# A seven-product second layer on all four experts of a fused attention and mixture-of-experts kernel on one Trainium2 core

## Chip, core and metric

The kernel runs on one core of one Trainium2 chip. The metric is the device time of one execution in microseconds (us), taken as the median of several executions. Executions of one kernel agree within about half a per cent. An experiment is always timed against the kernel before on the same chip in the same rounds. Its ratio is the mean time of its fast runs over the mean time of the fast runs of the kernel before of the same rounds, so it is not quite the ratio of the medians that I quote. A 95% interval stands beside it.

The *granted clock* is the share of PE's full clock that it was given.

The engines are called PE (TensorE: matmuls), DVE (VectorE), ACT (ScalarE), POOL (GpSimd) and SP (SyncE, which issues loads and stores). PE accumulates into PSUM banks, and DVE and ACT drain them.

## The reference

```python
def phi(x): return np.where(x > 0, x, np.exp(x) - 1.0) + 1.0     # elu + 1

q_p, k_p = phi(q), phi(k)                     # q, k, v: 8 batches x 8 heads x 576 tokens x 64
kv  = einsum('bhsd,bhse->bhde', k_p, v);  z = sum(k_p, axis=2)
x   = einsum('bhsd,bhde->bhse', q_p, kv) / (einsum('bhsd,bhd->bhs', q_p, z) + 1e-6)
x   = x.transpose(0, 2, 1, 3).reshape(4608, 512)
p   = domain_probs / domain_probs.sum(-1)
out = sum over 4 experts e of  p[:, e] * (relu(x @ w1[e]) @ w2[e])   # 512 -> 1024 -> 512
```

## The kernel before

Tokens are worked on in nine tiles of 512: each batch of 576 gives 512, and the eight left-over groups of 64 make up the last tile. A *unit* is one expert on one tile. Tile 0 and the first unit of tile 1 use plain matmuls. The other 31 units run in a software pipeline. Their first layer is cut into 2x2 sub-matrices and computed with **seven products instead of eight** (Strassen's scheme in Winograd's form). The price is sums of sub-matrices: of weights on DVE once, and of tokens on POOL for each tile. The second layer has the same scheme, but only on experts 0 and 2. I take the reason to be room: its three weight sums for each expert, 128x1024 fp16 each in the trace, take SBUF.

```python
SE = (0, 2)                                  # experts whose layer 2 is seven-product
...
def hidden_sums(h):                          # POOL: four sums for each half of the hidden units
    hs = pm.tile([P, 3, 2, NH], FP16, tag="hs", bufs=2, name="hs")
    nc.gpsimd.tensor_tensor(out=hs[:, 0], in0=a21, in1=a22, op=AO.add)
    ...
class Block:                                 # half a unit of layer 1: seven products in seven slots
    def p1(self):
        self.b = self.bank("b")
        self.products(self.b, ..., True)
        self.u1 = self.copy("u1", 1)         # ACT copies the bank to SBUF
    def p2(self):
        s2 = self.bank("s")                  # a bank of its own
        self.products(s2, ..., True)
        add_relu(self.h[:, :, 0, 0:NH], s2, self.u1)     # DVE: relu(bank + u1)
    ...
def phi_act(self, name, g, part=0, parts=1):
    ee = pa.tile([P, HG * CM * D], FP16, tag="phie", bufs=2, name="ee")  # exp goes to SBUF
    nc.scalar.activation(eeh, src, AF.Exp)
    if self.b > 2:
        nc.scalar.activation(dsth, src, AF.Identity, bias=1.0)           # x+1 on ACT
def phi_dve(self, name, g, part=0, parts=1):
    if self.b > 2:                           # one DVE instruction: min(max(x+1, 1), exp)
        nc.vector.scalar_tensor_tensor(out=dst, in0=dst, scalar=1.0, in1=ee, op0=AO.max, op1=AO.min)
    else:                                    # two: max(x+1, 1), then min with exp
        nc.vector.tensor_scalar(dst, src, 1.0, 1.0, AO.add, AO.max)
        nc.vector.tensor_tensor(out=dst, in0=ee, in1=dst, op=AO.min)
...
# in the pipeline, for each unit
if e in SE:
    l2 = [(layer2_product, j, e, hT, hss, p, i) for p in (2, 5, 1, 6, 7, 3, 4) for i in range(2)]
else:
    l2 = [... layer2_part ...]               # 32 plain matmuls of 512 columns, four DVE accumulations
```

Attention of the next batch (phi, kv, the division) is sprinkled between the products of a tile. So tile 1 carries the attention of the third batch (`b == 2`), and the last two tiles carry none.

## Time and profile before

| kernel before | |
|---|---|
| time before | 517.59 us median (515.88 to 517.7) |
| profiled execution, span | 514.0 us |
| PE busy | 96% |
| matmul work on PE, from start-to-start spacing | 487 us |
| PE stall between first and last matmul | 19 us |

From the page's first three parts: the header, busy time by engine, then PE's row and the granted clock in 40 slices of the span (9 means 90% or more). The fifth line is the chain that ended last.

```profile
span 514.0 us, 9987 instructions
PE 495.8 (96%) x3815; PEld 356.8 (69%) x3815; DVE 342.5 (67%) x676; ACT 289.0 (56%) x564; POOL 198.0 (39%) x207
PE   6899989999999999999999999999999999999996
PEclk9999999999999999999999999999999999999998
PE 85%; ACT 6%; DVE 3%; issue 2%; DMA 2%; POOL 0%; SPq 0%; DVEq 0%; ACTq 0%
```

PE is the bound: it is busy nearly everywhere. The two 6s at the ends are the start of the attention and the last stores.

Busy time includes the overlap of pipelined matmuls (the page gives a 512-column matmul a length of 379 ns), so I work with the spacing of starts. A long uninterrupted stretch of plain layer-2 matmuls is the cleanest ruler. This is the chain of waits in the last microseconds, with start, length and the number of instructions:

```profile
502.05 6.92 PE py L476 x32
```

This is 6.92 / 32 = 0.216 us for a matmul of 512 columns. The median spacing for 256 columns in this trace is 0.109 us. Everything above that spacing I call *stall*; where the records show the granted clock at half, I count the doubling apart as *clock* (eight matmuls of 256 columns took 1.71 us at half clock and 0.87 at full in the trace after).

In tile 1 PE waits for almost nothing; this is the whole answer of the wait view for PE in that stretch:

```profile
engine line waited for: us in total, times, longest us
PE psum_nl L380 <- DMA ql<-qlp: 0.5, 1, 0.5
```

Three groups of the page that the change touches: plain layer 2 (672 matmuls), the seven-product ones with a right-hand side from the weights (360), and the DVE add-ReLU after product 2 (`CUSTOM_DVE_ANT_0` is the page's name for the kernel's `add_relu`). Columns: line, engine, operation, out<-in, shape, count, busy us, mean ns, idle before.

```profile
L476 PE MATMUL py<-w,h 128*128 128x512 f16 x672 | 183.6, 379 | 0.3 <-DVE acc L467 0.3
L556 PE MATMUL py<-w,h 128*128 128x256 f16 x360 | 53.8, 272 | 2.8 <-ACT acc L465 2.7
L606 DVE CUSTOM_DVE_ANT_0 h<-ps,u 128x512 f16<-128x512 f32 x62 | 42.4, 684 | 6.5 <-PE ps L622 3.4
```

### The profile page before, as it was taken

The page shows a single profiled execution, that of the slowest core. Times are in us where ns is not written, and L with a number is a line of the kernel's source. Part 1 is how long each engine was busy: PE and PEld are TensorE (multiplying, and loading weights), DVE is VectorE, ACT ScalarE, POOL GpSimd, SP SyncE. Part 2 cuts the span into 40 slices and gives each one's busy share as a digit, 9 for nine tenths or more (in the row PEclk, how much of TensorE's full clock was granted, in tenths as well). Part 3 has the DMA queues.
Part 4 walks back from the last instruction along what each step waited for, and adds up shares of the span by engine and source line. Part 5 has one row for each costly group of instructions (what it writes and reads, how often), then busy time and mean ns, then how long its engine had stood idle before and what let it go on. Part 6 is the DMA issues. An engine that isn't in the chain of part 4 may idle for free.

```text
span 514.0 us, 9987 instructions
## 1 busy us (share of the span) xinstructions
PE 495.8 (96%) x3815; PEld 356.8 (69%) x3815; DVE 342.5 (67%) x676; ACT 289.0 (56%) x564; POOL 198.0 (39%) x207
## 2 busy tenths in 40 slices
PE   6899989999999999999999999999999999999996
PEld 2444445668787777778786868687778787878782
DVE  5614674689856885777677867687669555755573
ACT  5752465863876395737583668357843354335430
POOL 3522313016260736055423733372427251824240
PEclk9999999999999999999999999999999999999998
DMA  9999927573426334433435251523132110011003
GB/s 266 200 208 207 265 83 230 147 200 77 142 107 149 55 102 149 110 80 98 151 84 119 65 180 62 129 40 122 41 47 48 38 47 0 1 42 43 0 2 84
DMA packets 80193, 54.22 MB, mean 105 GB/s; under 512 B 45488, under 2 KB 73136, under 8 KB 80144
## 3 DMA queue, kind: packets, MB, share of 16 engines
q1 hardware_dynamic: 71104, 41.64, 30.5%
q0 software_dynamic: 9040, 11.93, 12.1%
q8 instruction: 30, 0.49, 0.4%
q14 instruction: 19, 0.16, 0.1%
HBM read 45.16 MB, written 9.44 MB: 106 GB/s over the span
## 4 chain that ended last, share of the span: by engine, by line
PE 85%; ACT 6%; DVE 3%; issue 2%; DMA 2%; POOL 0%; SPq 0%; DVEq 0%; ACTq 0%
PE py L476 27%; PE pb L622 19%; PE py L556 15%; PE pe L622 10%; PE ph L421 6%; PE ps L622 5%; ACT ee L226 2%; PE psum_kv L323 1%; ACT qp L228 1%; PE psum_nd L363 1%; DVE x_sb L346 1%; DMA rawb<-in_v_dram 1%; ACT acc L465 1%; DVE acc L467 1%; ACT u L633 1%
## 5 line engine op out<-in xcount | busy, mean ns | idle before, releaser
L476 PE MATMUL py<-w,h 128*128 128x512 f16 x672 | 183.6, 379 | 0.3 <-DVE acc L467 0.3
L467 DVE SCALAR_TENSOR_TENSOR acc<-py,p_sb,acc 128x256 f32<-128x256 f32 (+1 forms) x230 | 128.9, 567 | 41.3 <-PE py L556 24.4
L633 ACT COPY u<-pb 128x512 f32<-128x512 f32 x186 | 109.1, 588 | 79.6 <-PE pb L622 79.3
L606 DVE CUSTOM_DVE_ANT_0 h<-pe,u 128x512 f16<-128x512 f32 x124 | 85.3, 688 | 80.4 <-ACT u L633 47.4
L530 POOL TENSOR_TENSOR hs<-h 128x512 f16<-128x512 f16 x30 | 34.6, 1155 | 235.3 <-DVE h L606 235.3
L622 PEld LDWEIGHTS <-w 128*128 128x128 f16 x992 | 95.5, 98 | 33.4
L622 PEld LDWEIGHTS <-s 128*128 128x128 f16 x744 | 71.7, 98 | 24.8
L476 PEld LDWEIGHTS <-h 128*128 128x128 f16 x672 | 65.4, 98 | 30.1 <-issue 0.4
L666 ACT ACTIVATE h<-pb 128x512 f16<-128x512 f32 x62 | 37.1, 598 | 73.6 <-PE pb L622 73.4
L622 PE MATMUL pb<-tt,w 128*128 128x256 f16 x496 | 74.4, 273 | 0.0
L556 PE MATMUL py<-w,h 128*128 128x256 f16 x360 | 53.8, 272 | 2.8 <-ACT acc L465 2.7
L556 PEld LDWEIGHTS <-h 128*128 128x128 f16 x480 | 46.8, 98 | 10.3 <-issue 3.9
L606 DVE CUSTOM_DVE_ANT_0 h<-ps,u 128x512 f16<-128x512 f32 x62 | 42.4, 684 | 6.5 <-PE ps L622 3.4
L226 ACT ACTIVATE ee<-rawb 128x512 f16<-128x512 f32 (+1 forms) x54 | 37.1, 691 | 6.2 <-DMA rawb<-in_q_dram 6.0
L465 ACT ACTIVATE acc<-py,p_sb 128x256 f32<-128x256 f32 (+1 forms) x64 | 32.5, 507 | 12.2 <-PE py L556 6.7
L556 PEld LDWEIGHTS <-hs 128*128 128x128 f16 x360 | 35.2, 98 | 4.5 <-issue 0.3
L421 PE MATMUL ph<-xT,w 128*128 128x512 f16 x160 | 37.3, 379 | 0.8 <-ACT xT L400 0.7
L622 PE MATMUL pb<-tt,s 128*128 128x256 f16 x248 | 37.2, 273 | 0.0
L622 PE MATMUL pe<-tt,s 128*128 128x256 f16 x248 | 37.2, 273 | 0.0
L556 PE MATMUL py<-t,hs 128*128 128x256 f16 x240 | 35.9, 273 | 0.0
L531 POOL TENSOR_TENSOR hs<-hs,h 128x512 f16<-128x512 f16 x30 | 34.6, 1154 | 2.4
L532 POOL TENSOR_TENSOR h<-h 128x512 f16<-128x512 f16 x30 | 34.7, 1155 | 0.0
(97 smaller groups left out, 565.3 us busy)
## 6 DMA issues: line engine op xcount, KB each, us to landing
out_dram<-acc SPq DMA_DIRECT2D x32, 256.0 KB, 2.4
w<-in_moe_w_dram POOLq DMA_DIRECT2D x14, 512.0 KB, 19.8
rawb<-in_v_dram SPq DMA_DIRECT2D x13, 512.0 KB, 5.0
rawb<-in_q_dram SPq DMA_DIRECT2D x13, 512.0 KB, 3.9
rawb<-in_k_dram SPq DMA_DIRECT2D x13, 512.0 KB, 4.6
w<-in_moe_w_dram POOLq DMA_DIRECT2D x4, 256.0 KB, 6.8
rawb<-in_q_dram POOLq DMA_DIRECT2D x2, 512.0 KB, 6.1
rawb<-in_k_dram POOLq DMA_DIRECT2D x2, 512.0 KB, 4.7
```

The lines of the kernel that those rows point to most:

```text
L226: nc.scalar.activation(eeh, src, AF.Exp)
L421: nc.tensor.matmul(out=ph, lhsT=w1_sb[e][:, dc, fj * P : (fj + 1) * P], rhs=xT_of(j)[:, dc], start=(dc == 0), stop=(dc == DC - 1),)
L465: nc.scalar.activation(acc, ps, AF.Identity, scale=pscal)
L467: nc.vector.scalar_tensor_tensor(out=acc, in0=ps, scalar=pscal, in1=acc, op0=AO.mult, op1=AO.add)
L476: nc.tensor.matmul(out=py, lhsT=rows(hT, fj)[:, ns * P : (ns + 1) * P], rhs=w2_sb[e][:, fj, :], start=(fj == 0), stop=(fj == FC - 1),)
L530: nc.gpsimd.tensor_tensor(out=hs[:, 0], in0=a21, in1=a22, op=AO.add)
L532: nc.gpsimd.tensor_tensor(out=a21, in0=a11, in1=a21, op=AO.subtract)
L556: nc.tensor.matmul(out=ps, lhsT=lhsT(k), rhs=rhs[:, k], start=first and k == 0, stop=k == FH - 1, skip_group_check=True,)
L606: nc.vector._custom_dve(TENSOR_ADD_SAT, out=out, in0=ps, in1=u, s0=BIG, s1=0.0)
L622: nc.tensor.matmul(out=ps[:, kk], lhsT=lk(kc), rhs=rhs[:, kc], start=first and kk == 0 and kc == 0, stop=kc == 1, skip_group_check=True,)
L633: nc.scalar.copy(u, self.b)
L666: nc.scalar.activation(self.h[:, :, 1, 0:NH], self.b, AF.Relu)
```

## The change

The intent is to use the seven-product layer 2 on experts 1 and 3 too. The two further sets of weight sums need SBUF, and by my estimate they would not fit alone. So three companions make room and lighten DVE:

- Layer 1's first product is copied from PSUM to PSUM; product 2 accumulates on the copy, and ACT's ReLU replaces DVE's add-ReLU. This frees an SBUF buffer and the "s" banks.
- The exponential of phi goes to PSUM, into the freed "s" banks. In the third batch x+1 moves from DVE to ACT (`b > 2` becomes `b >= 2`).
- Loads come in halves (256 KB instead of 512 KB) through six buffers.

All positions in the pipeline are set anew, as fractions of a slot.

```diff
-    SE = (0, 2)
+    SE = (0, 1, 2, 3)
+    NRAW = 6
-            ee = pa.tile([P, HG * CM * D], FP16, tag="phie", bufs=2, name="ee")
-            if self.b > 2:
-                nc.scalar.activation(dsth, src, AF.Identity, bias=1.0)
+            if self.b >= 2:
+                nc.scalar.activation(dst..., src, AF.Identity, bias=1.0)
+                ee = aps([P, HQ * CM * D], FP32, "psum_ee")
+            else:
+                ee = pm.tile([P, HQ * CM * D], FP16, tag="hs0", bufs=2, name="ee")
...  (Block)
-            self.u1 = self.copy("u1", 1)
+            self.e5 = self.bank("e")
+            nc.scalar.copy(self.e5, self.b)
         def p2(self):
-            s2 = self.bank("s")
-            self.products(s2, lambda k: a_block(self.e, 0, 1, k), x[:, 2:4, 0:NH], True)
-            add_relu(self.h[:, :, 0, 0:NH], s2, self.u1)
+            self.products(self.e5, lambda k: a_block(self.e, 0, 1, k), x[:, 2:4, 0:NH])
+            nc.scalar.activation(self.h[:, :, 0, 0:NH], self.e5, AF.Relu)
...  (schedule)
-            if e in SE: ... (2, 5, 1, 6, 7, 3, 4) ...   else: plain layer 2
+            for d in range(2):
+                for i in range(4):
+                    put_at(at + HSUM[d][i], hsum, d, i)
+            for m in range(14):
+                put_at(at + L2AT[m], layer2_product, j, e, hT, hss, L2ORD[m // 2], m % 2)
-                for i, slot in enumerate((9, 12, 23, 25)):
-                    put(slot, weight_sums2, 2, i)
+                for m, pos in enumerate(WS2):            # eight sums, experts 2 and 3, in tile 1
+                    put(pos, weight_sums2, 2 + m // 4, m % 4)
...  (cut: half-size loads, single hidden and token sums, sorted work list, the position tables;
      layer 2's products in the order 2, 5, 1, 6, 3, 7, 4; layer 1's product 5 after product 2)
```

## The prediction

> **What bounds the kernel now.** TensorE. The profile's first part gives PE 495.8 of 514.0 us (96%); the chain of waits is 85% PE. From tile 1 on the loop is periodic (53.85 us per tile in the timeline). Spacing the matmuls by start time, a 512-column matmul costs 0.216 us and a 256-column one 0.109 us[...]. On that footing the matmuls fill 487 us and only about 19 us is stall: some 13 us before 110 us, about 1.1 us per steady tile, almost nothing in the last two tiles. Only fewer or cheaper matmuls can help much. The windows show DVE about 74%, ACT 60%, POOL 42% in the steady stretch 110 to 310 us.

> **What the change does.**
> 1. Experts 1 and 3 get the seven-product layer 2 in tiles 1 to 8: 16 units, each 56 matmuls of 256 columns (6.11 us) for 32 of 512 (6.91 us). 16 x 0.79 = 12.7 us of PE removed. All on the critical path: the whole gain.
> 2. Per such unit it adds eight hidden sums on POOL (1.11 us apart back to back) and 14 small accumulations on DVE (0.39) for four large (0.66).
> 3. Layer 1's first product is copied PSUM to PSUM, product 2 accumulates on it, and an ACT ReLU (about 0.48 us spacing) replaces a DVE add-ReLU (0.60): 62 move from DVE to ACT.
> 4. phi's exp lands in PSUM: DVE's min then has one SBUF input[...]. Duration of the min about unchanged (0.68).
> 5. Loads halved in size, positions retimed.

> Estimated load per 51.5-us tile after, from these spacings: POOL 40 us (78%), DVE 38 (74%), ACT 35 (69%). All below PE, which still bounds; but [...]a product's reader has about two slots of 0.87 us, so a few short PE stalls will appear. New coupling: the PSUM-to-PSUM copy waits until DVE has drained the same "e" bank.

> **What it costs.** Tail: the last unit ran 32 direct matmuls back to back. Now it waits for four serial POOL sums (about 4.5 us), only partly covered by PE work: about 1.4 us given back. Front: within 1 us. Steady stalls: between -3 and +4 us in total.

> **Sum.** 517 - 12.7 + 1.4 + 0.5 = about 506 us, range 502.5 to 511. Faster by over 2%: 0.56; within 2%: 0.42; slower by over 2%: 0.02. The 2% line (about 507) is mid-range.

> **What would show it.** Right: matmuls of 512 columns on the direct layer-2 line fall from 672 to 160, seven-product matmuls rise from 720 to about 1,616; tile period 51.2 to 52.5 us; POOL about 75 to 80% in the steady stretch; [...]product 2's DVE ReLU group gone; PE idle of 1 to 2 us in the last 15 us.
> Wrong: PE waiting on POOL sums or on DVE accumulations several times per tile; a tile period over 53 us.

> **What would make it wrong.** POOL falling behind so that products 5 to 3 wait; DVE's small accumulations or ACT's longer queue delaying release of PSUM banks; or, on the good side, the retiming removing most of the old stalls (then 502 to 503).

## More of the kernel before

Below, "faster" as a verdict means by over 2%.

The experiments did not all run in the same rounds; where I subtract the medians of two of them, the rounds differ. The tiles' lengths come from one profiled execution of each kernel.

Busy time in two stretches: tile 1 of the pipeline, and 100 us of its steady state. The first two numbers are the stretch and its length, and the three at the end are granted clock, DMA share and GB/s.

```profile
89.21:126.86 37.65, 37.03 (x294) 26.69 (x293) 31.05 (x70) 23.39 (x46) 10.18 (x9) 1.00 0.57 148
210.00:310.00 100.00, 99.37 (x817) 76.28 (x817) 73.69 (x146) 60.91 (x125) 41.93 (x41) 1.00 0.42 111
```

The columns are PE, PE's weight loads, DVE, ACT, POOL.

## The result

The changed kernel took **513.75 us** (513.41 to 516.1, five runs), and the kernel before of the same rounds took 516.34 (515.88 to 517.7, five runs). The ratio is 0.9947 [0.9923, 0.9971]: faster by half a per cent. It lies outside the predicted range of 502.5 to 511.

The page of the profiled execution after, with the lines that answer to those above. This execution is the slowest of the five (516.1 us; its mean clock was 0.987, the others' 0.990 to 0.995).

```profile
span 514.3 us, 11256 instructions
PE 489.0 (95%) x4199; PEld 397.7 (77%) x4199; DVE 366.0 (71%) x787; ACT 324.2 (63%) x647; POOL 345.8 (67%) x340
PE   6799978889999999999999999999999999999994
PEclk9799999998999999999999999999999999999998
PE 80%; DVE 8%; ACT 5%; DMA 2%; issue 2%; SPq 2%; DVEq 0%; ACTq 0%
```

PE is less busy in slices 6 to 9 (about 64 to 116 us), and the clock row has two dips that the kernel before does not show: about 16 to 23 us, and 115 to 118.5 us. The chain gives DVE more.

```profile
93.73:136.83 43.10, 38.07 (x305) 28.70 (x304) 31.31 (x63) 31.21 (x63) 20.41 (x17) 0.96 0.52 116
210.00:310.00 100.00, 100.00 (x952) 89.59 (x951) 80.14 (x175) 73.54 (x153) 79.61 (x76) 1.00 0.42 110
```

The steady stretch runs as hoped: PE has no gap at all although POOL is now at 80%. Tile 1 is what became bad: 43.10 us instead of 37.65, with *less* matmul work in it. PE's waits in tile 1, the four largest:

```profile
PE pb L673 <- ACT h L717: 1.4, 1, 1.4
PE py L611 <- DVE acc L518: 1.2, 3, 0.8
PE pb L673 <- ACT u L684: 0.9, 2, 0.5
PE psum_nl L431 <- DVE kp L286: 0.8, 1, 0.8
...
```

These are waits for the two draining engines. The groups that answer to those of before, and the new ReLU on ACT:

```profile
L527 PE MATMUL py<-w,h 128*128 128x512 f16 x160 | 38.4, 379 | 0.8 <-DVE acc L518 0.8
L611 PE MATMUL py<-w,h 128*128 128x256 f16 x744 | 107.4, 274 | 0.7 <-DVE acc L518 0.2
L699 ACT ACTIVATE h<-pe 128x512 f16<-128x512 f32 x62 | 37.0, 598 | 53.2 <-PE pe L673 52.6
```

So the operations moved as the prediction listed: 512 of the 672 plain matmuls are gone, and 2.7 us of waits on ACT with them.

Where the time went, stage by stage, from the starts of the first matmul of each stage in the two profiled executions:

| stage | before, us | after, us | difference |
|---|---|---|---|
| start to first expert matmul | 17.75 | 20.13 | +2.38 |
| to the first pipelined block | 71.46 | 73.61 | +2.15 |
| tile 1 | 37.65 | 43.10 | **+5.45** |
| tiles 2 to 8, to the last block | 364.12 | 350.04 | **-14.08** |
| last block to last matmul | 17.61 | 20.66 | +3.05 |
| after the last matmul | 5.46 | 6.79 | +1.33 |
| span | 514.05 | 514.33 | +0.28 |

By kind, over the same pair: matmul work -12.5 (487.2 to 474.7), stall +7.1 (19.3 to 26.4), clock +4.4 (0 to 4.4), end +1.3. The saving arrived; as much was given back outside the steady stretch. The split between stall and clock is not one between two causes: experiment 8 shows that in tile 1 the one takes the place of the other. The profiled execution after is the slowest of its five, and the one before, by its span, the fastest; so the medians differ by 2.6 us and the profiled pair by almost nothing.

### The profile page after: what moved, and what is told of

It is laid out like the page before. It is cut to its first block, busy times and chain, and to the rows that moved or that the text cites. A ratio compares the mean times of both kernels' runs of the same rounds, so it can differ in the third digit from the quotient of the medians.

```text
span 514.3 us, 11256 instructions
## 1 busy us (share of the span) xinstructions
PE 489.0 (95%) x4199; PEld 397.7 (77%) x4199; DVE 366.0 (71%) x787; ACT 324.2 (63%) x647; POOL 345.8 (67%) x340
## 4 chain that ended last, share of the span: by engine, by line
PE 80%; DVE 8%; ACT 5%; DMA 2%; issue 2%; SPq 2%; DVEq 0%; ACTq 0%
PE py L611 34%; PE pb L673 19%; PE pe L673 14%; PE ph L472 5%; PE py L527 5%; DVE acc L518 3%; DVE x_sb L397 2%; PE psum_kv L374 1%; DMA rawu<-in_v_dram 1%; SPq L239 1%; DMA qT<-qp 1%; PE psum_nd L414 1%; DVE h L657 1%; ACT u L684 1%; ACT vp L295 1%
## 5 line engine op out<-in xcount | busy, mean ns | idle before, releaser
L518 DVE SCALAR_TENSOR_TENSOR acc<-py,p_sb,acc 128x256 f32<-128x256 f32 (+1 forms) x390 | 184.0, 487 | 62.0 <-PE py L611 48.9
L583 POOL TENSOR_TENSOR hs<-h 128x512 f16<-128x512 f16 x62 | 72.0, 1161 | 67.7 <-DVE h L657 67.7
L611 PE MATMUL py<-w,h 128*128 128x256 f16 x744 | 107.4, 274 | 0.7 <-DVE acc L518 0.2
L585 POOL TENSOR_TENSOR hs<-hs,h 128x512 f16<-128x512 f16 x62 | 71.7, 1156 | 24.8 <-PE py L611 22.2
L611 PEld LDWEIGHTS <-hs 128*128 128x128 f16 x744 | 71.8, 98 | 11.3 <-issue 2.9
L611 PE MATMUL py<-t,hs 128*128 128x256 f16 x496 | 74.4, 272 | 1.2 <-DVE acc L518 1.0
L589 POOL TENSOR_TENSOR hs<-h,hs 128x512 f16<-128x512 f16 x62 | 71.7, 1157 | 3.2 <-PE py L611 3.2
L587 POOL TENSOR_TENSOR h<-h 128x512 f16<-128x512 f16 x62 | 72.2, 1164 | 0.0
L699 ACT ACTIVATE h<-pe 128x512 f16<-128x512 f32 x62 | 37.0, 598 | 53.2 <-PE pe L673 52.6
L693 ACT COPY pe<-pb 128x512 f32<-128x512 f32 x62 | 35.9, 579 | 46.7 <-PE pb L673 43.1
L527 PE MATMUL py<-w,h 128*128 128x512 f16 x160 | 38.4, 379 | 0.8 <-DVE acc L518 0.8
L516 ACT ACTIVATE acc<-py,p_sb 128x256 f32<-128x256 f32 (+1 forms) x64 | 31.4, 508 | 7.5 <-PE py L527 4.2
```

Source lines behind the costliest of these rows:

```text
L518: nc.vector.scalar_tensor_tensor(out=acc, in0=ps, scalar=pscal, in1=acc, op0=AO.mult, op1=AO.add)
L527: nc.tensor.matmul(out=py, lhsT=rows(hT, fj)[:, ns * P : (ns + 1) * P], rhs=w2_sb[e][:, fj, :], start=(fj == 0), stop=(fj == FC - 1),)
L583: nc.gpsimd.tensor_tensor(out=hs[0], in0=a21, in1=a22, op=AO.add)
L585: nc.gpsimd.tensor_tensor(out=hs[1], in0=hs[0], in1=a11, op=AO.subtract)
L587: nc.gpsimd.tensor_tensor(out=a21, in0=a11, in1=a21, op=AO.subtract)
L589: nc.gpsimd.tensor_tensor(out=hs[3], in0=a12, in1=hs[1], op=AO.subtract)
```

## The experiments

The theory: the seven-product layer 2 delivers, and the time is given back in separate places that the companions and the new positions brought, tile 1 above all, then the tail, the front, and PE's clock. Rival A: the seven-product layer itself costs, by its POOL sums and small DVE accumulations. Rival B: the copies and exponentials in PSUM cost.

Each experiment is an edit of the changed kernel. All eighteen were reported correct by the comparison with the reference.

### 1. Back to experts 0 and 2 (e1_se02)

```diff
-    SE = (0, 1, 2, 3)
+    SE = (0, 2)
+            if e not in SE:
+                for m in range(16):
+                    put_at(at + 3.5 + m * 0.87, layer2_part, j, e, m // 4, hT, m % 4, 4)
+                continue
...  (cut: the weight sums of experts 1 and 3 are left out, four of the eight in tile 1 among them)
```

> The changed kernel with experts 1 and 3 put back to the direct layer 2, every other part of the change kept. First theory (the saving of TensorE work is delivered in the steady tiles and given back at three places: the front with its smaller loads, tile 1, the tail): the steady tile goes from 51.4 back to about 53.0 us, which costs 12.7 us; the tail and part of tile 1 recover 5 to 6; the front stays at its late 24 us. Total 518 to 522 us, slower than the kernel before. Rival (the losses come from the seven-product layer 2 itself, which loads DVE and POOL everywhere): all give-backs vanish with it, front too, and the time is that of the kernel before, 515 to 517.

Measured: 523.73 us (523.46 to 524.78), ratio 1.0145 [1.0126, 1.0164]. With the experts as before and everything else of the change kept, the kernel is 7.6 us *slower* than before, and 10 us slower than the full change. That is beyond both ranges that were expected. Tile 1 is 41.78 us. So the give-back is not the price of the seven products (rival A): it comes with the companions and positions. (The positions here are those that were set for the seven products; how much plain layer 2 suffers from them was not tested.) In tile 1 DVE was busy only 25.8 us here, and ACT 31.4, as in the full change.

### 2. Both PSUM parts undone (e2_u1phi)

```diff
-                ee = aps([P, HQ * CM * D], FP32, "psum_ee")
+                ee = pm.tile([P, HQ * CM * D], FP16, tag="phie", bufs=2, name="ee")
-            nc.scalar.copy(self.e5, self.b)
+            self.u1 = self.copy("u1", 1)
+            s2 = self.bank("s")
-            nc.scalar.activation(self.h[:, :, 0, 0:NH], self.e5, AF.Relu)
+            add_relu(self.h[:, :, 0, 0:NH], s2, self.u1)
...  (cut: the same for the left-over groups, and what makes room)
```

For room, u1 is fp16 here, the probabilities share a buffer, and five load buffers stand instead of six.

> The changed kernel with the two PSUM parts undone together (they share banks and could not be undone apart in this direction): layer 1's first product is copied to SBUF again and added by DVE, the exp lands in SBUF again; to make room, five raw buffers for six and the first-product copy in 16 bits. If these parts were needed so that the other engines keep up: DVE gets 62 add-ReLUs back (about 1.2 us per unit, 74% to about 83% busy), its min has two SBUF inputs beside a busy POOL, steady tile 52 to 53.5 us and 3 to 10 us slower in all. If they were only a matter of taste: within 1 us of the changed kernel and the steady tile still 51.4.

Measured: 545.11 us (544.6 to 546.56), ratio 1.056 [1.0538, 1.0582]. The steady tile went from 51.42 to 57.0 us, while the tile without attention stayed at 48.91. The steady stretch and PE's waits in it:

```profile
210.00:310.00 100.00, 93.20 (x865) 80.81 (x864) 86.85 (x172) 58.32 (x119) 72.07 (x64) 1.00 0.40 98
PE py L611 <- DVE acc L518: 6.5, 12, 1.0
```

DVE is at 87% and PE waits for its accumulations. Rival B falls: without the PSUM parts the seven products could not be fed. That is 31 us for what looked like companions, where 3 to 10 us were expected.

### 3. Only the exponential back in SBUF (e11_phi)

```diff
-                ee = aps([P, HQ * CM * D], FP32, "psum_ee")
+                ee = pm.tile([P, HQ * CM * D], FP16, tag="phie", bufs=2, name="ee")
...  (cut: the same for the left-over groups; five load buffers instead of six, for room)
```

> The changed kernel with only the exp back in SBUF (five raw buffers for six to make room); the first product still copied PSUM to PSUM. Undoing both PSUM parts cost 31 us. If most of that was the 62 add-ReLUs returned to DVE: this run loses 0 to 8 us, from min operations lengthened beside POOL. If most was the exp (two SBUF inputs beside POOL): 15 us or more, and the min's mean goes from 0.69 to over 1.0 us.

Measured: 527.36 us (526.86 to 528.84), ratio 1.0213 [1.0192, 1.0234], so 13.6 us more than the full change (against the kernel before, the verdict at 2% is "unclear"). This lies between the two expected ranges. DVE's minimum of phi by group, here (first three lines) and then in the changed kernel:

```profile
L286 DVE SCALAR_TENSOR_TENSOR qp<-qp,ee 128x512 f16<-128x512 f16 x24 | 27.5, 1147 | 2.4 <-ACT ee L279 2.4
L286 DVE SCALAR_TENSOR_TENSOR kp<-kp,ee 128x512 f16<-128x512 f16 x24 | 18.7, 781 | 5.1 <-ACT ee L279 5.0
L329 DVE SCALAR_TENSOR_TENSOR kl<-kl,el 64x256 f16<-64x256 f16 x12 | 11.6, 965 | 0.5 <-ACT el L317 0.4
```

```profile
L286 DVE SCALAR_TENSOR_TENSOR kp<-kp,psum_ee 128x512 f16<-128x512 f16 x24 | 16.3, 680 | 5.0 <-ACT psum_ee L279 5.0
L286 DVE SCALAR_TENSOR_TENSOR qp<-qp,psum_ee 128x512 f16<-128x512 f16 x24 | 16.3, 679 | 2.9 <-ACT psum_ee L279 2.9
L329 DVE SCALAR_TENSOR_TENSOR kl<-kl,psum_el 64x256 f16<-64x256 f16 x12 | 5.0, 414 | 0.5 <-ACT psum_el L317 0.5
```

The same instruction with both inputs in SBUF took 1147, 781 and 965 ns beside a busy POOL; with one input in PSUM it took 679, 680 and 414. In the kernel before, with both inputs in SBUF and POOL at 42%, it took 682; but there only 5 of these 40 minimums met a POOL sum at all, each for 0.13 us. In this run the 5 of 48 that met none took 693 ns, and the 43 that met one 995 on average. In the changed kernel 43 of 48 met one as well, and the 31 that lay wholly under one took 675 to 689 ns. So the minimum was longer beside a POOL sum with both inputs in SBUF, and not with one of them in PSUM. The exponential itself took 604 ns into PSUM and 629 into SBUF. The copy alone was not undone with the exponential left in PSUM, because the two would share the "s" banks. What that part is worth, about 18 us, is only the difference of experiments 2 and 3, which ran in different rounds and also differ in how they make room.

### 4. The tail: plain layer 2 for the last unit (e3_tail)

```diff
+            if n == len(units) - 1:
+                put_at(at + 1, weight_sums2, e, 3)      # restores the weights' changed block
+                for m in range(16):
+                    put_at(at + 4.5 + m, layer2_part, j, e, m // 4, hT, m % 4, 4)
+                continue
```

> The changed kernel, only the very last unit (last tile, expert 3) with the direct layer 2 as before; one weight block is put back first by one DVE subtraction. First theory: the stretch from the start of the last block to the end goes from 27.4 us back to about 23 to 24, total 3 to 4 us less (510 to 511). Rival that the tail only inherits delays from before: no more than 1 us less.

Measured: 512.1 us (511.27 to 513.34), ratio 0.9918 [0.9895, 0.9941]. From the last block to the end it took 24.84 us (19.82 + 5.02) instead of 27.45, a little less than the expected gain; the total, too, fell by less than expected. The chain at the end of the changed kernel shows why:

```profile
499.01 0.61 PE py L611 x4
499.63 0.03 issue
499.65 0.49 DVE acc L518
500.14 0.04 issue
500.19 0.61 PE py L611 x4
```

Four matmuls, then a DVE accumulation that frees the bank, then four matmuls, each pair 1.17 us. With no layer 1 of a next unit between them, the small products are paced by DVE. There is no POOL in this chain: the hidden sums, which the prediction feared, were in time. In experiment 4 PE runs through:

```profile
499.90 4.98 PE py L527 x23
```

### 5. The tail: stores issued by two engines (e4_stores)

```diff
-                nc.sync.dma_start(
+                (nc.sync if u == 0 else nc.scalar).dma_start(
```

> The changed kernel, only every second one of the last tile's eight output stores issued from the ACT queue in place of the SyncE queue. In the changed kernel the last accumulation ends 6.0 us before the end, before the change 4.3, because the stores become ready together and are issued one after the other, 0.64 us each. If that is it: 1.2 to 1.8 us less. If the landing of the transfers sets the end: nothing.

Measured: 513.38 us (512.32 to 514.22), ratio 0.9934 [0.9913, 0.9955]. The end after the last matmul fell from 6.79 to 5.04 us, as it did in experiment 4. In the changed kernel the eight last stores of 128 KB become ready nearly together, and SP issued them about 0.64 us apart (0.60 to 0.69 but for one). That one of the eight took 1.85 us to issue in the profiled execution; in experiment 8's, with one issuer and no such long one, the end came 5.5 us after the last matmul. So part of the 1.75 us may be chance. It helps to make them ready one after the other (experiment 4) or to issue them from two engines (here). The total moved too little for the rounds to show it.

### 6. and 7. The front: whole loads for the first batch (e5_front), more buffers for exp (e6_ee)

```diff
-        for (n, i), home in zip(ORDER, homes):
-            b0.load(n, i, home=home)
+        if i % 2 == 0 and (n, i) in (("q", 0), ("k", 0), ("v", 0), ("q", 2)):
+            b0.load_pair(n, i)                          # 512 KB, as before
...
```

> The changed kernel with the loads of the first batch merged again where a full-size home is free (q, k, v of the first half and q of the second as 512 KB loads; 8 loads of q, k, v in place of 12). In the trace of the changed kernel a load costs SyncE 0.5 to 0.6 us to issue whether it is 256 or 512 KB, and the last v lands at 15.3 us for 14.0 before the change. If issue time delays the front: last v about 14 us, first layer-1 matmul about 1 us earlier, 1 to 3 us less in all (the upper end if a half-clock window goes with it). If the front is late for another reason (the exp tiles, the clock): within 0.5 us.

```diff
-                ee = pm.tile([P, HQ * CM * D], FP16, tag="hs0", bufs=2, name="ee")
+                ee = pm.tile([P, HQ * CM * D], FP16, tag=EE[next(een) % 3], bufs=2, name="ee")
```

> The changed kernel with the exp tiles of the first two batches spread over six buffers (three tags) in place of two. In the changed kernel ACT's exp waits there for DVE's min to free a buffer (3.8, 2.5 and 0.9 us of ACT waits), and the second batch's K x V product then waits 2.8 us for the ones-column and v cast behind a load that waits for that exp. If so: the stretch from the first layer-1 matmul to the first block shrinks from 69.7 to about 68.5, the front by up to 1 us; 1.5 to 3 us less. If the waits are covered anyhow: within 0.5 us.

Measured: 514.75 us (513.74 to 515.21), ratio 0.9967 [0.9946, 0.9988], and 513.51 us (512.61 to 514.86), ratio 0.9942 [0.9917, 0.9967]. Both are misses: neither is told from the changed kernel. The first expert matmul came at 19.05 and 19.85 us. Without any half-clock stretch in the front (the profiles of experiments 4 and 6) the first expert matmul is still 1.3 to 1.4 us later than before and the first pipelined block 2.1 to 2.3 us. What makes it so stays open.

### 8. The front: longer runs of filler matmuls (e12_warm)

The kernel has filler matmuls between the first attention steps (`warm`). This experiment has ten more of them.

```diff
-        warm(4) ... warm(1) ... warm(3) ... warm(3)
+        warm(9) ... warm(2) ... warm(5) ... warm(5)
```

> The changed kernel with ten more warm-up matmuls in the front where TensorE idles. Every run of the changed kernel has one to three 3.4 us windows at half clock before 130 us, the kernel before has none. If the idle front causes the first one: no window before 24 us in this run and 0.5 to 1.7 us less. If the windows come whatever the front does: no change. The added matmuls themselves can cost up to 0.5 us.

Measured: 513.46 us (512.52 to 513.88), ratio 0.9942 [0.9923, 0.9961]. The profiled execution had no half-clock stretch in the front, and its first expert matmul came at 19.27 us instead of 20.13, but the median did not move. One execution says little: the profile of experiment 4, with the old fillers, had none in the front either (19.17 us). Over all profiles of the changed kernel and its variants, a half-clock stretch lies before 60 us in 9 of the 12 with the old fillers and in 2 of the 7 with the longer ones. So fewer fall in the front.

What goes before them is seen in tile 1 of the changed kernel, in three consecutive stretches of it:

```profile
108.20:111.60 3.40, 3.40 (x30) 2.50 (x28) 1.08 (x2) 3.29 (x8) 3.37 (x3) 1.00 0.40 131
111.60:115.10 3.50, 1.68 (x15) 1.19 (x14) 2.19 (x4) 3.50 (x8) 0.91 (x2) 1.00 0.51 150
115.10:118.50 3.40, 3.40 (x19) 2.42 (x17) 2.42 (x5) 3.05 (x8) 3.32 (x4) 0.50 0.41 104
```

PE is busy 1.68 of 3.50 us in the second, while ACT is busy all of it; then the clock is halved for 3.41 us, although PE is busy throughout. No single wait of PE in tile 1 was over 1.4 us: partly idle was enough.

The clock records of this trace, from 5.84 us on, hold 10.24 us at full clock, 6.83 at half, 92.16 at full and 3.41 at half: 3, 2, 27 and 1 times 3.413 us. I cut the profile, up to the last matmul, at these steps. Two of the pieces at full clock were followed by half clock: in 12.67 to 16.08 us PE was busy 1.72 us (50%), in 111.66 to 115.07 us 1.59 (46.5%). In all the others it was busy 54% or more. In the kernel before no piece was followed by half clock, and the least busy one (64.17 to 67.58 us) had 1.71 us (50%).

In tile 1 the halved clock hardly costs anything. In experiments 5 and 7, whose tile 1 is that of the changed kernel, no such stretch fell into it, and yet it is as long. This is experiment 5, to compare with the 43.10 us above:

```profile
93.66:136.63 42.97, 36.80 (x305) 27.81 (x304) 31.27 (x63) 31.07 (x63) 20.44 (x17) 1.00 0.51 115
```

Its stall there is 8.7 us instead of 7.1: PE waits for the draining engines anyway, at half clock or at full. (Tile 1 is 43.08 to 43.10 us in the four profiles of it with such a stretch, and 42.97 and 42.96 in the two without.) In the front it does cost: the first pipelined block starts at 91.5 us in experiment 4's profile, without a stretch, and at 93.2 to 94.4 in the four profiles of the same front with two or three.

### 9. Tile 1: the weight sums moved out (e7_ws)

```diff
+        for m in range(8):                              # before the pipeline starts
+            weight_sums2(2 + m // 4, m % 4)
-                for m, pos in enumerate(WS2):
-                    put(pos, weight_sums2, 2 + m // 4, m % 4)
```

> The changed kernel with the eight weight-block subtractions of experts 2 and 3 moved out of tile 1 to just before it, where DVE idles 3.8 us. In tile 1 they take up to 1.5 us each for 0.68 where POOL's sums run beside them, and TensorE waits for DVE's accumulations there. If DVE in tile 1 is the cause: tile 1 (first block to tile 2) goes from 43.1 to 40.5 to 41.5 us. If ACT's burst of phi is: at most 0.5 us less.

Measured: 511.54 us (511.14 to 511.82), ratio 0.9901 [0.9883, 0.9919]. Tile 1 is 41.1 us instead of 43.1, and nothing was given back where the sums went. No half-clock stretch fell into it in this execution. Against the profiles of the unchanged tile 1 without one (experiments 5 and 7: 43.0 us, stall 8.7) it is 1.8 us shorter, all of it stall (6.8).

### 10. Tile 1: later positions for the attention's queries (e8_attn0)

```diff
-            q=(16.1, 17.6, 19.1, 20.5),  qd=(16.1, 18.4, 21.0, 22.6),  lq=23.8, lqd=24.3, qT=23.8,
+            q=(16.1, 18.6, 21.1, 23.6),  qd=(16.9, 19.4, 21.9, 24.4),  lq=25.8, lqd=26.3, qT=24.6,
```

> The changed kernel with phi(q) of the third batch (four pairs of activations in tile 1) spaced 2.5 slots apart in place of 1.5. At 111.7 us a first product of the changed kernel waits 1.5 us for a ReLU that stands behind such activations in ACT's queue, and a half-clock window follows. If ACT's burst is the cause: tile 1 from 43.1 to 40.5 to 42 us, and no half-clock window near 115 us. If DVE's weight sums are: within 0.5 us.

Measured: 514.94 us (514.36 to 515.85), ratio 0.9969 [0.9949, 0.9989]; tile 1 43.8 us, with 9.5 us of stall. A miss: spreading the same work out did not shorten the stall (8.7 us without it).

### 11. Tile 1: the third batch's x+1 back on DVE (e9_b2dve)

```diff
-            if self.b >= 2:
+            if self.b > 2:
                 nc.scalar.activation(dst..., src, AF.Identity, bias=1.0)
+            if self.b >= 2:
                 ee = aps([P, HQ * CM * D], FP32, "psum_ee")
```

> The changed kernel, only the third batch (whose attention runs in tile 1) makes its x + 1 on DVE again as before the change, not on ACT; its exp still lands in PSUM. The change had moved ten such operations, about 5.5 us, to ACT in tile 1, where TensorE then waits for ACT's copies and ReLUs five times (3.7 us). If ACT is the bound there: those waits go, tile 1 from 43.1 to 40 to 41.5 us. If DVE, which also makes eight weight sums there, is as full: DVE waits take their place and tile 1 stays above 42.5 us.

Measured: 512.94 us (512.62 to 513.24), ratio 0.9929 [0.9913, 0.9945]. Tile 1 is 41.0 us, without a half-clock stretch, and its stall 6.7 us; against the same two profiles, 2 us less.

### 12. Both together, with one step moved (e10_wsb2)

Experiments 9 and 11, and the left-over division of the second batch from position 7.5 to 10.5.

> The run before together with the weight sums moved ahead of tile 1 (which alone gave 41.1 us for tile 1), and the second batch's leftover product moved three slots later, off a moment when the PSUM banks that it shares with the exp are taken. If ACT's added work and DVE's weight sums are together the cause of tile 1: 36 to 38 us there (34.3 us of matmuls), 508 to 509.5 us in all. If something else holds it: over 40 us.

Measured: 512.04 us (511.57 to 512.53), ratio 0.9912 [0.9895, 0.9928]; tile 1 42.4 us, stall 6.4 and 1.7 more at half clock. A clear miss: the two savings of 2 us did not add. Either the moved step spoiled it, or the two share one bound.

### 13. to 15. All give-backs undone, three ways (e13_sum_ws, e14_sum_both, e15_sum_b2)

Experiment 13 joins numbers 4, 5, 8 and 9. Experiment 14 adds number 11 with the left-over step at its old place. Experiment 15 is 14 without the moved weight sums.

> The give-backs undone together: the eight weight sums of experts 2 and 3 before the pipeline starts instead of inside tile 1, the last unit's layer 2 as 32 direct matmuls, the last stores split over two issuing engines, longer warm-up runs in the front. Theory (the give-backs are separate places on TensorE's own chain): tile 1 as in the run with the weight sums alone (41.1 us against 43.1), end after the last matmul about 4 us (5.0 with either half alone), last block to last matmul 19.8 instead of 20.7, no half-clock window before 60 us; together about 4 to 5 us, so 508.5 to 510 us, ratio 0.984 to 0.988. Rival (the savings share one cause, or each moves the wait somewhere else, as when two were put together in the run of the weight sums with the third batch): no better than 511.5 us, the weight-sum run alone.

> As the run before it, and the third batch's x+1 back on the vector engine, but the left-over denominator step kept at its place (the run that combined these before had moved it and lost). Theory (moving that step was what spoiled the combination): tile 1 about 38 to 40 us, total 506.5 to 508.5 us, ratio 0.981 to 0.984, which is over 2% or at its edge. Rival (the two share one bound in tile 1, the drain of PSUM by the vector engine and the scalar engine together): tile 1 stays at 41 us and the total within 0.5 us of the run before it.

> The same with the third batch's x+1 on the vector engine, but the weight sums left in tile 1 as the change has them. Theory of separate causes: tile 1 41.0 us, total 509 to 510.5 us. Rival (one shared bound in tile 1): the same total as both runs beside it within 0.5 us.

Measured in the same rounds (before 516.06 us):

| | us | ratio | tile 1 |
|---|---|---|---|
| e13_sum_ws | 508.98 (507.98 to 509.71) | 0.9851 [0.9819, 0.9883] | 41.3 |
| e14_sum_both | 509.45 (508.97 to 509.78) | 0.9860 [0.9835, 0.9884] | 42.1 |
| e15_sum_b2 | 509.54 (508.71 to 510.73) | 0.9864 [0.9836, 0.9893] | 41.0 |

Experiment 13 is as the theory had it: with four places undone together the median is 4.8 us below that of the changed kernel (513.75, other rounds). The rival that was set against 14 is right: the two changes in tile 1 share a bound, and the moved step was innocent. Tile 1 in 13 and in 14:

```profile
92.16:133.41 41.25, 37.35 (x305) 28.73 (x304) 29.51 (x61) 31.22 (x63) 19.66 (x17) 0.96 0.54 121
91.75:133.87 42.12, 36.78 (x306) 28.61 (x305) 34.95 (x72) 26.20 (x52) 20.08 (x17) 0.96 0.52 119
```

Putting x+1 on DVE took 5.0 us from ACT and gave DVE 5.4. The sum of the two engines is the same, 60.7 and 61.2 us, and so is tile 1. In the kernel before this sum is 31.05 + 23.39 = 54.4 us.

### 16. The disputed work taken away (e16_noadd)

On top of 13. The third batch's phi is the smaller of exp and 1. Its output is wrong, which doesn't matter for the time. (The comparison with the reference still passed; it is not fine enough to see this in one of eight batches.)

```diff
-                nc.scalar.activation(dst.rearrange("p c h d -> p h c d"), src, AF.Identity, bias=1.0)
+                if self.b > 2:
+                    nc.scalar.activation(dst.rearrange("p c h d -> p h c d"), src, AF.Identity, bias=1.0)
...
+            if self.b == 2:
+                nc.vector.tensor_scalar(dst, ee, 1.0, 0.0, AO.min, AO.max)
```

> Wrong results on purpose: the third batch's x+1 is left out altogether (phi becomes the smaller of exp and 1), on top of the run with the weight sums before the pipeline. It takes eleven scalar-engine instructions of 0.42 to 0.64 us, about 6.6 us, out of tile 1 and adds nothing to the vector engine. Theory (in tile 1 the scalar and vector engines together have too much to do in bursts, so moving work between them does not help but removing it does): tile 1 from 41.3 to between 36 and 39 us, waits of TensorE on the scalar engine's readers mostly gone; total 505 to 507.5 us. Rival (the order of the queues or the positions in tile 1, not the amount of work): tile 1 stays at 40.5 us or above, total within 1 us of 509.

Measured: 505.14 us (504.15 to 506.49), ratio 0.978 [0.9748, 0.9812], "unclear" at 2%. Tile 1:

```profile
92.85:129.64 36.79, 35.12 (x306) 27.86 (x304) 29.11 (x61) 26.05 (x52) 19.66 (x17) 1.00 0.55 136
```

Tile 1 is 36.8 us, below that of the kernel before. Stall and half clock together fell from 7.0 to 2.5 us. ACT had 5.2 us less to do and DVE the same. So it was the amount of draining work in this tile that held PE up: with less of it, the same order stalls for only 1.2 us more than the kernel before.

### 17. and 18. The cheaper phi for the third batch, correct (e17_b2_sbuf, e18_b2_hs3)

Why does moving x+1 to ACT add work? The mean times of one part of phi in tile 1 tell. Before: exp 635 ns on ACT, then 420 and 427 ns on DVE, 1.48 us in all. After: 602 and 638 ns on ACT, 688 ns on DVE, 1.93 us. The minimum of two fp16 inputs in SBUF took 427 ns; with the exponential in PSUM, as fp32, the same operation took 692 ns (in experiment 11), 1.6 times as long. For the later batches nothing is lost, because there the single instruction took 682 ns before and takes 680 after. So, on top of 13, the third batch gets its old form back:

```diff
-            if self.b >= 2:      # exp in PSUM, x+1 on ACT
+            if self.b > 2:
                 ...
             else:                # exp in SBUF, two DVE instructions
-                ee = pm.tile([P, HQ * CM * D], FP16, tag="hs0", bufs=2, name="ee")
+                ee = pm.tile([P, HQ * CM * D], FP16, tag="hs3" if self.b == 2 else "hs0", bufs=2, name="ee")
```

The second edit is in 18 alone.

> A correct kernel: on top of the run with the four places undone, the third batch's phi is computed as the kernel before does it, with exp to fp16 in SBUF and two vector-engine instructions of about 0.42 us each, instead of exp in PSUM, x+1 on the scalar engine (0.64) and a minimum of 0.69 from PSUM; the exp shares the buffers of the hidden sums. Theory (the amount of work on scalar and vector engine in tile 1): scalar 31.2 to 26 us, vector 29.5 to about 31 us, their sum from 60.7 to about 57; tile 1 from 41.3 to 38 to 40 us, total 506 to 508 us. Rival (a version that is bound by order, or the new wait for the hidden sums' buffers, costs the same): tile 1 at 41 us or more, total 509 us or more.

> The same with the third batch's exp in the buffers of the last of the hidden sums instead of the first. If waiting for the hidden sums' buffers costs anything in the run before, this one differs from it by over 0.5 us in tile 1; if not, the two agree within 0.5 us.

Measured: 17 took 508.01 us (507.63 to 509.16), ratio 0.9837 [0.9816, 0.9857]; 18 took 509.49 us (507.64 to 510.79), ratio 0.986 [0.9838, 0.9882]. Tile 1 of 17:

```profile
92.52:131.70 39.18, 35.68 (x305) 27.86 (x304) 31.79 (x72) 26.21 (x52) 19.57 (x17) 1.00 0.54 128
```

DVE and ACT together are 58.0 us and tile 1 is 39.2, as the theory had it; 17 is the best correct kernel, by 1.6% over the kernel before. Its lead over 13 (0.9837 against 0.9851) is within the intervals; the tile's length is the evidence, not the total. In 18, tile 1 is 41.4 us with a half-clock stretch (1.4) and 5.7 us of stall, against 4.9 in 17, and a single wait of 1.9 us for ACT's copy that 17 does not have (0.2). The instructions are the same, but DVE was busy 2.4 us longer: its x+1 and minimum of q took 954 and 806 ns instead of 493 and 615. So which buffer the exponential shares matters as well, and by as much as 17 gained over 13 in tile 1. Busy time is not the amount of work alone.

Tile 1 in one table. Work on PE is 34.3 us in all of them but the kernel before (36.4). The length of the tile is work, stall and what was lost to half clock; read the last two together, since the one takes the place of the other (experiment 8).

| | ACT, us | DVE, us | sum | PE stall, us | half clock, us | tile 1, us |
|---|---|---|---|---|---|---|
| before | 23.4 | 31.1 | 54.4 | 1.3 | 0 | 37.7 |
| e16_noadd | 26.1 | 29.1 | 55.2 | 2.5 | 0 | 36.8 |
| e17_b2_sbuf | 26.2 | 31.8 | 58.0 | 4.9 | 0 | 39.2 |
| e18_b2_hs3 | 26.3 | 34.2 | 60.5 | 5.7 | 1.4 | 41.4 |
| e7_ws | 31.1 | 29.5 | 60.6 | 6.8 | 0 | 41.1 |
| e13_sum_ws | 31.2 | 29.5 | 60.7 | 5.3 | 1.7 | 41.3 |
| e10_wsb2 | 26.3 | 34.5 | 60.8 | 6.4 | 1.7 | 42.4 |
| e14_sum_both | 26.2 | 35.0 | 61.2 | 6.2 | 1.7 | 42.1 |
| e9_b2dve, e15_sum_b2 | 25.8 | 36.1 | 61.9 | 6.7 | 0 | 41.0 |
| e4_stores, e6_ee (tile 1 as after) | 31.0 | 31.3 | 62.3 | 8.7 | 0 | 43.0 |
| e8_attn0 | 31.1 | 31.3 | 62.3 | 9.5 | 0 | 43.8 |
| after | 31.2 | 31.3 | 62.5 | 7.1 | 1.7 | 43.1 |

Up to 58 us, stall and half clock together are at most 4.9 us. From 60.5 to 62.5 us they are 6.7 to 8.8, with either split of the work between the two engines, and 9.5 with other positions. So the busy time sets the level roughly, and the split, positions and buffers move it by up to about 2 us. Experiment 1 stands outside this: DVE 25.8, ACT 31.4, sum 57.1, and yet 6.7 us of stall. So the sum is no law; whether the positions, not fitted to plain layer 2, are the reason there was not tested.

## Why the prediction was wrong

**"16 x 0.79 = 12.7 us of PE removed. All on the critical path": right.** Matmul work fell by 12.5 us, and tiles 2 to 8 by 14.1. Their stalls even fell, from 5.4 to 2.5 us: the old waits of the seven-product layer on ACT (2.7 us) went with the new order of products. The period came out at 51.4 us, inside the predicted 51.2 to 52.5.

**Mechanisms of the steady state: right.** The predicted loads (POOL 78%, DVE 74%, ACT 69%) were 80, 80 and 74%. (The prediction's counts of seven-product matmuls, 720 and 1,616, leave out a group of 120; the pages have 840 and 1,736. The copy of the first product took 579 ns into PSUM, against 588 for the copies to SBUF before.) What experiment 3 measured afterwards is 995 ns for the minimum beside a POOL sum with both inputs in SBUF, against 675 to 689 under one with one input in PSUM. The copy and the exponential are not optional: 31 us go without them.

**"Steady stalls: between -3 and +4 us in total": this is the step that failed most.** For tiles 2 to 8 it holds (-3.0). But it took the whole pipeline as steady. Tile 1 is not. There the third batch's attention is packed into three units, layer 2's eight weight sums fell on DVE, and x+1 had moved to ACT in a form that costs both engines together 0.45 us more for each of eight parts. Tile 1's stall rose by 5.8 us, and with the clock it was 5.45 us longer although its work fell by 2.1. Experiment 16 shows the cause by taking the work away; 17 agrees with a correct kernel, though 18 shows that its gain also hangs on a buffer. The diff shows both edits (`b >= 2`, eight sums instead of four), and a stretch of the before trace shows that DVE was already 82% busy there; I averaged over the steady stretch and did not cost this tile.

**PE's clock: left out.** The profiled execution lost 4.4 us to half-clock stretches, against none before its last microseconds; other executions lost less. In that execution it followed stretches in which PE was busy 50% and 46.5% (1.72 and 1.59 of 3.41 us). So it was part of the price of the front; in tile 1 it took the place of stall.

**"Front: within 1 us": too small.** The first expert matmul came 1.3 to 2.9 us later in the profiles, and the start-up to the first block took another 2.15 us in the profiled pair; about 2.7 us of this was clock in that execution. Experiments 6 and 7 did not find the reason for the rest; it is open.

**"about 1.4 us given back" in the tail: wrong in mechanism and size.** It was 3.05 us up to the last matmul and 1.33 after it. PE waited for DVE's accumulations, not for POOL's sums, and eight stores queued at one issuer. Experiment 4 undid 0.84 + 1.77 us of this.

The sum for the medians: 516.3 - 12.5 (work) leaves 503.8, and the kernel took 513.75. Experiment 17, with the tail, the stores and tile 1 mended, took 508.0: it got back 5.7 of the missing 10 us, across different rounds. The largest pieces left in its profile are the front and 4.9 us of stall in tile 1.

## What to carry to other kernels

Price a change for the stage with the most work on the draining engines, not only for the steady stretch: the tile in which a software pipeline starts up can give back much of what the others gain. Moving an operation between two engines that are both needed there may help little (here 2 us alone, and nothing once the weight sums were moved), and a move can make it longer, so add up both engines' time before and after. Where PE was busy for less than about half of a 3.41 us stretch (50% and 46.5% in the profile after; a stretch of 50% in the profile before was spared), its clock was halved for the next one. Whether that costs anything must be measured: it lengthened the front here, but not tile 1, where PE waited for other engines anyway.
